# A two-layer expert kernel: the second layer of all three token blocks by seven half-width products

## The chip, the cores and the metric

The program runs on one core of a Trainium2 chip. The metric is device time in microseconds (us) from launch to end, the median of several executions; one more execution was recorded by the hardware profiler, and what is read below comes from that one. The engines are called TensorE (PE in the profile; its weight loads PEld), VectorE (DVE), ScalarE (ACT), GpSimd (POOL) and SyncE (SP, which issues the transfers).

## The reference

Gated linear attention over 4 x 8 heads gives 3072 tokens of width 384; a softmax gate, balanced by eight Sinkhorn rounds, weights eight two-layer experts for every token.

```python
logits = x @ w_gate;  P = np.exp(logits - logits.max())
...                                   # 8 rounds of row and column scaling
for e in range(8):
    h = np.maximum(x @ w1[e], 0.0)    # 384 -> 1024
    out += P[:, e:e + 1] * (h @ w2[e])  # 1024 -> 384
```

All products are made of float16 matmuls: each factor is split into a high and a low part, and a product is three matmuls (high x high, low x high, high x low).

## The kernel before, in words

The first third of the program (to about 490 us) computes the attention, the gate, and experts 0 and 1 in the plain way. The change lies in the rest: experts 2 to 7, in 48 periods. A period (`ORDER`) is one expert, one half of the inner width (512 of 1024) and one of four groups of 768 tokens.

*First layer.* A fast matrix-product scheme forms the period's 3 x 3 by 3 x 2 block product from 15 products (`SLOTS`), six matmuls of 256 columns each, in six PSUM banks kb_A to kb_F. Between products ScalarE copies banks out (`copy`, tiles cp), VectorE adds them into others (`add`, `init`, `sum`), and in the end the banks hold the hidden values, which ScalarE rectifies into float16 high parts (kh, kah, kgh) and VectorE or GpSimd turn into low parts (kl, kal, kgl). `EVENTS` tells after which product each of these stands; numbers of 15 and over belong to the next period. Two 256-token pairs are also summed into kr and kf, the left factors (kg) of the fast scheme of the second layer.

*Second layer.* Of three token blocks, 0 and 1 are `paired`: two 128-token halves at once by seven half-width (192-column) products from sums of the left factors (ka, kg, kh) and of the weights (k2, k2s), 42 matmuls. Block 2 is `plain`: 24 matmuls of 384 columns. Results lie in kxps and kyps; VectorE combines them (both, acc), or ScalarE scales them (yt) and GpSimd adds them into acc. These matmuls are dealt out between the first-layer products of a later period by a budget (`drain`), `LAG` products behind.

*Weights.* While one half's four token groups run, the next half's weights are loaded and prepared: `prepare_w1` (sums k1s on GpSimd, high parts k1h on ScalarE, low parts k1l on VectorE, a maximum wmx on VectorE) and `prepare_w2` (k2s, k2h, k2l, k2sl likewise), each step tied to a product by a list of numbers. The period in which k1l and k2l are formed is called heavy below, the other light; they alternate.

Every engine's order is fixed by the order in which the code records its instructions (`pin` and `mm`), so an instruction that waits holds up all behind it on its engine.

Of the kernel before, what the change touches and what calls it, by code (L numbers as in the profile page):

```python
# [258 lines left out]
def fast(ctx, tc, qkf, vbd, wg, w1, w2, out, flag):  # L259
# [784 lines left out]
    def prepare_w2(e, j, plain_first=False):  # L1044
        raw = raw_weights(e, 2, j)
        yield

        def maxima_():
            pin(nc.vector.tensor_reduce(out=wmx[:, 1, 4 * e + j:4 * e + j + 1], in_=raw.rearrange("p a f -> p (a f)"), axis=AX.X, op=ALU.max, apply_absolute_value=True))

        def lows():
            for g in range(2):
                pin(nc.vector.scalar_tensor_tensor(out=wl[:, g], in0=raw[:, g], scalar=W2S, in1=wh[:, g], op0=ALU.mult, op1=ALU.subtract))
# [448 lines left out]
```

## Time and profile before

| | us |
|---|---|
| median of three runs | 1511.97 (1510.23 to 1512.18) |
| profiled execution | 1511.74, its span 1510.0 |
| TensorE busy | 1477.1 |
| VectorE busy | 1282.7 |
| ScalarE, GpSimd busy | 1002.8, 968.4 |

A span runs from the first to the last instruction. In a row of the order of time stand the start, the duration, engine and line, the operation, output and inputs by the program's names, and their shapes; neighbours on one engine may overlap by some tens of nanoseconds, so the distance of two starts is what one costs. "x2" merges two neighbours.

### The profile page before, as it was taken

How to read it: one execution, taken by the hardware profiler on the slowest of the kernel's cores; microseconds unless marked ns; L12 is line 12 of the kernel's file. 1: busy time of each engine (PE TensorE's matmuls, PEld its weight loads, DVE VectorE, ACT ScalarE, POOL GpSimd, SP SyncE). 2: the span in 40 equal slices, each digit the busy share in tenths (PEclk: the TensorE clock that was granted, in tenths of full speed). 3: DMA queues.
4: the chain of work that ended last, by engine and by line, in shares of the span. 5: the costliest groups of instructions: out<-in, count | busy, mean ns of one | idle time of the engine just before them, and what ended most of it. 6: DMA issues, size and time to landing. Idle time of an engine off the chain costs nothing.

```text
span 1510.0 us, 37891 instructions
## 1 busy us (share of the span) xinstructions
PE 1477.1 (98%) x15185; PEld 1213.1 (80%) x15185; DVE 1282.7 (85%) x2352; ACT 1002.8 (66%) x2103; POOL 968.4 (64%) x1154
## 2 busy tenths in 40 slices
PE   7999999999999999999999999999999999999997
PEld 5788877666665788888888888888888888888885
DVE  8878888986676888989999999889899989888765
ACT  6655555654344777777777777777777777777663
POOL 1254444446429456888888887888777777777543
PEclk9999999999999999999999999999999999999999
DMA  8455654541001101222112221111111011000011
GB/s 280 113 133 131 139 129 117 138 121 35 22 27 46 39 12 49 59 60 55 55 47 64 64 64 34 42 54 43 32 33 33 23 33 33 22 12 12 7 59 66
DMA packets 82794, 95.85 MB, mean 63 GB/s; under 512 B 49872, under 2 KB 66384, under 8 KB 82608
## 3 DMA queue, kind: packets, MB, share of 16 engines
q1 hardware_dynamic: 82608, 93.34, 22.2%
q8 instruction: 120, 1.97, 0.6%
q14 instruction: 66, 0.54, 0.1%
HBM read 69.53 MB, written 14.16 MB: 55 GB/s over the span
## 4 chain that ended last, share of the span: by engine, by line
PE 88%; DVE 7%; ACT 2%; issue 1%; POOL 1%; DMA 1%; DVEq 0%; POOLq 0%; ACTq 0%
PE kyps L287 21%; PE yps L287 13%; PE kxps L287 12%; PE hps L287 10%; PE kb_A L287 8%; PE kb_B L287 8%; PE kb_D L287 6%; PE kb_C L287 4%; PE kb_E L287 2%; PE kb_F L287 2%; PE kvps L287 1%; PE aps L287 1%; DMA w1r<-in_w_dram 1%; DVE kf L1375 1%; POOL k1s L1026 0%
## 5 line engine op out<-in xcount | busy, mean ns | idle before, releaser
L287 PEld LDWEIGHTS <-k1h 128*128 128x128 f16 x2880 | 282.1, 98 | 38.7 <-DVE kl L1392 0.5
L1220 POOL TENSOR_TENSOR acc<-acc,yt 128x384 f32<-128x384 f32 x175 | 203.2, 1168 | 105.7 <-ACT yt L1219 101.2
L1387 POOL TENSOR_TENSOR kgl<-kf,kgh 128x512 f16<-128x512 f32 x188 | 217.1, 1165 | 40.9 <-ACT kgh L1384 40.2
L1219 ACT ACTIVATE yt<-kyps,pes 128x384 f32<-128x384 f32 x175 | 103.7, 592 | 131.8 <-PE kyps L287 69.6
L287 PEld LDWEIGHTS <-kh 128*128 128x128 f16 x1536 | 147.3, 98 | 34.8 <-DVE acc L1212 1.5
L287 PEld LDWEIGHTS <-k1l 128*128 128x128 f16 x1440 | 141.1, 98 | 24.6 <-issue 3.6
L287 PEld LDWEIGHTS <-kgh 128*128 128x128 f16 x1536 | 144.3, 98 | 5.3 <-ACT kgh L1384 1.1
L287 PE MATMUL yps<-w2h,hl 128*128 128x384 f16 x384 | 125.5, 327 | 2.8 <-DVE hl L440 2.6
L287 PE MATMUL yps<-w2l,hh 128*128 128x384 f16 x384 | 125.4, 326 | 1.9 <-DVE w2l L359 1.9
L287 PE MATMUL kyps<-k2h,kh 128*128 128x384 f16 x384 | 125.2, 326 | 1.5 <-DVE acc L1212 1.2
L287 PE MATMUL yps<-w2h,hh 128*128 128x384 f16 x384 | 125.5, 327 | 0.2 <-ACT hh L437 0.2
L287 PE MATMUL kyps<-k2h,kl 128*128 128x384 f16 x384 | 125.2, 326 | 0.4 <-DVE kl L1392 0.4
L287 PE MATMUL kyps<-k2l,kh 128*128 128x384 f16 x384 | 125.2, 326 | 0.0
L287 PEld LDWEIGHTS <-w1h 128*128 128x128 f16 x1344 | 97.2, 98 | 34.0 <-issue 3.1
L1384 ACT ACTIVATE kgh<-kf 128x512 f16<-128x512 f32 x192 | 120.7, 629 | 3.6 <-DVE kf L1375 3.5
L1254 POOL TENSOR_TENSOR part<-part 128x192 f32<-128x192 f32 x96 | 57.3, 596 | 88.7 <-DVE kf L1375 61.1
L287 PEld LDWEIGHTS <-hh 128*128 128x128 f16 x768 | 74.6, 98 | 47.7 <-issue 2.5
L1353 ACT ACTIVATE cp<-kb_A 128x512 f32<-128x512 f32 x144 | 87.4, 607 | 21.9 <-PE kb_A L287 21.6
L287 PE MATMUL kyps<-k2sl,kgh 128*128 128x192 f16 x384 | 94.5, 246 | 0.0
L287 PE MATMUL kyps<-k2sh,kgl 128*128 128x192 f16 x384 | 94.5, 246 | 0.0
L287 PE MATMUL kyps<-k2sh,kgh 128*128 128x192 f16 x384 | 94.5, 246 | 0.0
L287 PEld LDWEIGHTS <-kl 128*128 128x128 f16 x768 | 75.1, 98 | 23.3 <-issue 5.3
(294 smaller groups left out, 5404.3 us busy)
## 6 DMA issues: line engine op xcount, KB each, us to landing
q<-in_qkf_dram SPq DMA_DIRECT2D x23, 672.0 KB, 5.1
vr<-in_vbd_dram SPq DMA_DIRECT2D x24, 384.0 KB, 3.6
k1r<-in_w_dram SPq DMA_DIRECT2D x24, 384.0 KB, 3.0
ys<-yr SPq DMA_DIRECT2D x48, 192.0 KB, 2.7
k2r<-in_w_dram SPq DMA_DIRECT2D x24, 384.0 KB, 3.1
yb<-ys SPq DMA_DIRECT2D x48, 192.0 KB, 2.6
out_dram<-acc SPq DMA_DIRECT2D x24, 192.0 KB, 1.9
w1r<-in_w_dram SPq DMA_DIRECT2D x8, 384.0 KB, 7.7
```

The lines of the kernel that those rows point to most:

```text
L287: ins = (nc.tensor.transpose if transpose else nc.tensor.matmul)(**kw)
L1219: pin(nc.scalar.activation(out=yt, in_=ps, func=AF.Copy, scale=p))
L1220: pin(nc.gpsimd.tensor_tensor(out=y, in0=y, in1=yt, op=ALU.add))
L1254: pin(nc.gpsimd.tensor_tensor(out=part[:, 1, :], in0=part[:, 1, :], in1=part[:, 2, :], op=ALU.add))
L1353: pin(nc.scalar.activation(out=fresh(ev[2]), in_=bk, func=AF.Copy))
L1375: pin(nc.vector.scalar_tensor_tensor(out=f[:, n], in0=bk[:, :, 128 * v:128 * v + 128], scalar=0.0, in1=other, op0=ALU.max, op1=op))
L1384: pin(nc.scalar.activation(out=hs['g', t][0][:, lo:hi], in_=hs['f', t][:, lo:hi], func=AF.Copy))
L1387: pin((nc.vector if tag == str(PERIODS - 1) else nc.gpsimd).tensor_tensor(out=hs['g', t][1][:, lo:hi], in0=hs['f', t][:, lo:hi], in1=hs['g ...
```

## The change

All three blocks of the second layer are `paired`; `plain` is gone. The seven products now stand in the schedule by number (five first-layer products to a block, `advance`), six products behind the first layer instead of two. The scheme inside a block is rewritten with two running sums instead of a GpSimd chain: three ScalarE copies into PSUM (kxps, kyps) or part, then four scaled adds of 192 columns into acc, or into yy and xx that GpSimd adds to acc; kxps takes a bank of its own. The first layer gets along with five banks, kb_A and kb_F of a period lying in one. The third block's left factors come from kb_D and kb_F (`hs`, `gs`, `gd`), and every kal is formed by VectorE from its bank (`gf`). The weights' tile k2 now holds seven half-width parts.

```diff
-PLAIN, PAIRED = (2,), (0, 1)
+PAIRED = (0, 1, 2)
+BY_POOL = (1,)
-LAG = 2
+LAG = 6
...
-    pk = ctx.enter_context(tc.tile_pool(name="pk", bufs=6, space=PSUM, reuse_waits="tile"))
+    pk = ctx.enter_context(tc.tile_pool(name="pk", bufs=1, space=PSUM, reuse_waits="tile"))
...
+        product(y0, None, (0, 0), start=True)
+        product(x1, (None, 0), (None, 0))
+        yield
+        move(x0, y0)
+        move(p2, x1, scale=scale(1))
+        yield
+        product(y0, (None, 2), (None, 2))
+        yield
+        move(x1, y0)
+        yield
+        product(x0, (1, 0), (1, 0), stop=True)
+        yield
+        yield
+        product(x1, (None, 1), (None, 1))
+        yield
+        out_x(0, x0)
+        add(yy[:, 1, :], x1, scale(1), p2)
+        yield
+        product(y0, (1, 1), (None, 3), stop=True)
+        product(x1, (None, 3), (1, 1), stop=True)
+        yield
+        add(yy[:, 0, :], y0, scale(1), p2)
+        out_x(1, x1)
...
-            at_all(n, (10, 12, 18, 22, 23, 26, 26, 27, 38) if n != 3 else (0, 2, 8, 12, 13, 16, 16, 17, 20), prepare_w2(e2, 2 * m2 + part // 2))
-        if 3 <= n:
+            at_all(n, (10, 22, 25, 26, 27, 29, 35, 38) if n != 3 else (0, 2, 8, 12, 13, 16, 17, 20), prepare_w2(e2, 2 * m2 + part // 2))
+        if n >= FIRST_READD:
...
+    def kbank(n, bk):
+        k = "AFEC".find(bk)
+        tag = bk if k < 0 else f"k{(max(k - 1, 0) + int(n)) % 3}"
+        return pk.tile([128, 2, 256], F32, name=f"kb_{n}_{bk}", tag=tag)
...
+    def advance(n, s):
+        k, j = divmod(n * PRODUCTS + s - LAG, 5)
+        k -= TT
+        if k >= 0 and not j and k < PERIODS * TT:
+            going.append(paired(k // TT, helped[k // TT], PAIRED[k % TT]))
+        if not going or j == 1 and len(going) == 1 and k < PERIODS * TT:
+            return lambda: None
+        block = going[0 if j == 1 else -1]
+        next(block)
```

The first place that the prediction speaks of is VectorE's order in a heavy period (the 24th), from the add into kb_B to the making of kb_F. Before:

```order
L1355 TENSOR_TENSOR kb_B<-kb_B,cp_0_16334 128x512
L1039 SCALAR_TENSOR_TENSOR k1l_1_16087<-k1s_1_16001,k1h_1_16086 128x640 x2
L1039 SCALAR_TENSOR_TENSOR k1l_1_16087<-k1r_1_15843,k1h_1_16086 128x256
L1039 SCALAR_TENSOR_TENSOR k1l_1_16087<-k1r_1_15843,k1h_1_16086 128x384
L1375 SCALAR_TENSOR_TENSOR kf_0_16370<-kb_A,kr_0_16373 128x256
L1381 SCALAR_TENSOR_TENSOR kal_0_16390<-kb_A,kah_0_16389 128x256
L1355 TENSOR_TENSOR kb_D<-kb_D,cp_7_16414 128x512
L1053 SCALAR_TENSOR_TENSOR k2l_1_16265<-k2r_1_16072,k2h_1_16264 128x384
L1358 TENSOR_TENSOR kb_F<-kb_D,cp_1_16288 128x512
```

And now, from behind the add into kb_B on:

```order
L1182 SCALAR_TENSOR_TENSOR yy_2_16895<-kyps_2_16892,pes,part_2_16894 128x192
L1182 SCALAR_TENSOR_TENSOR acc_8993<-kyps_2_16892,pes,acc_8993 128x192
L1039 SCALAR_TENSOR_TENSOR k1l_1_16728<-k1s_1_16583,k1h_1_16727 128x640
L1047 TENSOR_REDUCE wmx<-k2r_1_16754 128x1
L1039 SCALAR_TENSOR_TENSOR k1l_1_16728<-k1s_1_16583,k1h_1_16727 128x640
L1039 SCALAR_TENSOR_TENSOR k1l_1_16728<-k1r_1_16496,k1h_1_16727 128x256
L1039 SCALAR_TENSOR_TENSOR k1l_1_16728<-k1r_1_16496,k1h_1_16727 128x384
L1332 SCALAR_TENSOR_TENSOR kal_0_17090<-kb_A,kah_0_17089 128x256
L1182 SCALAR_TENSOR_TENSOR acc_9363<-kxps_0_17016,pes,acc_9363 128x192
L1182 SCALAR_TENSOR_TENSOR yy_0_17018<-kyps_0_17015,pes,part_0_17017 128x192
L1302 TENSOR_TENSOR kb_D<-kb_D,cp_7_17112 128x512
L1305 TENSOR_TENSOR kb_F<-kb_D,cp_1_16975 128x512
```

Two scaled adds of the third block stand ahead of the k1l, the second layer's maximum stands between them, two more adds stand ahead of kb_D, and k2l has gone further down.

The second place is VectorE right behind kb_F in the same period, up to the low part of kb_D. Before:

```order
L1375 SCALAR_TENSOR_TENSOR kf_0_16370<-kb_B,kr_0_16373 128x256
L1375 SCALAR_TENSOR_TENSOR kf_0_16370<-kb_B,kf_0_16370 128x256 x2
L1364 TENSOR_TENSOR cp_3_16501<-kb_D,cp_4_16212 128x512
L1392 SCALAR_TENSOR_TENSOR kl_1_0_16179<-kb_B,kh_1_0_16178 128x512
L1257 TENSOR_TENSOR both_1_16444<-kyps_1_16442,part_1_16443 128x192
L1355 TENSOR_TENSOR kb_C<-kb_C,cp_3_16501 128x512
L1392 SCALAR_TENSOR_TENSOR kl_1_2_16183<-kb_D,kh_1_2_16182 128x512
```

And now, from k2l on:

```order
L1064 SCALAR_TENSOR_TENSOR k2l_1_17124<-k2r_1_16754,k2h_1_17123 128x192
L1064 SCALAR_TENSOR_TENSOR k2l_1_17124<-k2r_1_16754,k2h_1_17123 128x384
L1302 TENSOR_TENSOR kb_C<-kb_C,cp_3_17223 128x512
L1182 SCALAR_TENSOR_TENSOR yy_1_17139<-kyps_1_17136,pes,part_1_17138 128x192
L1351 SCALAR_TENSOR_TENSOR kl_2_16863<-kb_D,kh_2_16862 128x512
L1326 TENSOR_TENSOR kr_2_17286<-kr_2_17286 128x256
L1323 SCALAR_TENSOR_TENSOR kr_2_17286<-kb_D,kr_2_17286 128x256
L1323 SCALAR_TENSOR_TENSOR kf_2_17318<-kb_D,kr_2_17286 128x256
L1323 SCALAR_TENSOR_TENSOR kf_2_17318<-kb_D,kf_2_17318 128x256
```

k2l stands here now, and four instructions on the third block's left factors (kr, kf) follow the low part of kb_D, three of them reading that bank.

The third place is GpSimd's order beside it. Before:

```order
L1387 TENSOR_TENSOR kgl_1_16233<-kf_1_16231,kgh_1_16232 128x512 x2
L1220 TENSOR_TENSOR acc_9256<-acc_9256,yt_0_1_16349 128x384
L1071 TENSOR_TENSOR k2s_1_16353<-k2r_1_16072 128x192 x2
L1074 TENSOR_TENSOR k2s_1_16353<-k2r_1_16072,k2s_1_16353 128x192 x2
L1291 TENSOR_TENSOR acc_9594<-acc_9594,yz_6_1_16394 128x384
```

And now:

```order
L1346 TENSOR_TENSOR kgl_22_2_17054<-kr_2_16908,kgh_22_2_17052 128x512
L1218 TENSOR_TENSOR acc_8993<-acc_8993,yy_2_16895 128x384
L1346 TENSOR_TENSOR kgl_22_2_17055<-kf_2_16938,kgh_22_2_17053 128x512
L1326 TENSOR_TENSOR kr_0_17071<-kr_0_17071 128x256
L1239 TENSOR_TENSOR acc_8993<-acc_8993,yz_2_2_17101 128x384
L1057 TENSOR_TENSOR k2s_1_17155<-k2r_1_16754 128x192 x2
```

The two kgl of the third block and a kr are new there, and the weights' sums k2s come later.

More of the change, by code (lines that the diff above doesn't have):

```diff
@@ L1223, in product @@
-        def product(out, t, left, right, start=False, stop=False):
+        p = psm.tile([128, DM], F32, name=f"kyps_{n}_{t}", tag="m")
+        q = pk.tile([128, DM], F32, name=f"kxps_{n}_{t}", tag="x")
+        x0, y0, x1 = q[:, 0:DH], p[:, 0:DH], p[:, DH:DM]
+        p2 = lp.tile([128, DH], F32, name=f"part_{n}_{t}", tag="part", bufs=2)
+        by_pool = t in BY_POOL and n < len(ORDER) - 1 and not new
+        xx, yy = (acc[b][:, v, t, :].rearrange("p (s d) -> p s d", s=2) for v in range(2))
@@ L1224, in product, with scale @@
+        if not new:
+            yy = rp.tile([128, 2, DH], F32, name=f"yy_{n}_{t}", tag="yraw", bufs=3)
+        if by_pool:
+            xx = rp.tile([128, 2, DH], F32, name=f"xx_{n}_{t}", tag="yraw", bufs=3)
+        def scale(v):
+            return pes[:, (2 * b + v) * TT + t, e:e + 1]
+        def product(out, left, right, start=False, stop=False):
             for c in range(2):
@@ L1441, in fast @@
         period(n)
[L1442 to L1453 removed]
+    for s in range(LAG + PRODUCTS + 2):
+        for ev in pending.pop(0) if pending else []:
+            event(*ev)
+        advance(PERIODS, s)()
+        if s > 7:
+            next(judged, None)
+    if going:
+        raise RuntimeError("a block was left")
     for _ in again:
```

307 lines of the change are left out of this document (108 added, 199 removed), and 12 rows, old and new, of the table EVENTS.

## The prediction

> **What bounds the kernel now.** I read the page's totals first, then busy time by stretch, then TensorE's waits, then VectorE's and TensorE's order of time through one period.
>
> ```profile
> span 1510.0 us, 37891 instructions
> PE 1477.1 (98%) x15185; PEld 1213.1 (80%) x15185; DVE 1282.7 (85%) x2352; ACT 1002.8 (66%) x2103; POOL 968.4 (64%) x1154
> ```
>
> ```profile
> core 0: us, PE busy (x) PEld busy (x) DVE busy (x) ACT busy (x) POOL busy (x), PEclk, DMA share, GB/s
> 485.00:600.00 115.00, 107.38 (x960) 88.80 (x959) 91.38 (x169) 80.59 (x167) 62.80 (x87) 0.99 0.13 39
> 841.45:862.53 21.08, 21.08 (x206) 18.51 (x204) 20.20 (x37) 17.26 (x38) 18.19 (x21) 1.00 0.14 39
> 862.53:882.76 20.23, 20.23 (x196) 17.66 (x194) 17.40 (x34) 14.65 (x31) 16.39 (x24) 1.00 0.25 79
> 700.00:1100.00 400.00, 399.23 (x3831) 349.40 (x3829) 360.29 (x676) 307.88 (x657) 327.68 (x402) 1.00 0.17 49
> 1485.00:1510.00 25.00, 14.09 (x136) 11.27 (x133) 15.49 (x37) 7.98 (x19) 7.98 (x10) 0.94 0.19 69
> ```
>
> From 700 to 1100 TensorE lacks 0.8 us in 400, so matmul pitch sets the time there. VectorE is at 90% on average, but unevenly: in the period 841.45 to 862.53, where low parts of new weights are formed (a heavy period), it is busy 20.20 us; in the next, a light one, 17.40. The two together last 41.3 us, 20.65 each. The reserve in a heavy period is what this forecast turns on.
>
> ```profile
> 852.43 0.27 PE L287 MATMUL kb_A<-xbh,k1h 128*128 128x256 f16 x1
> 853.09 0.33 PE L287 MATMUL kyps<-k2h,kh 128*128 128x384 f16 x1
> 853.90 0.27 PE L287 MATMUL kb_E<-xah,k1h 128*128 128x256 f16 x1
> 847.91 0.25 PE L287 MATMUL kxps<-k2sl,kgh 128*128 128x192 f16 x1
> 848.73 0.27 PE L287 MATMUL kb_D<-xah,k1h 128*128 128x256 f16 x1
> 861.25 0.27 PE L287 MATMUL kb_D<-xah,k1h 128*128 128x256 f16 x1
> ```
>
> Pitches by starts: six 256-column matmuls stand between the first two rows (0.66/6 = 0.109 us), five of 384 between the next (0.81/5 = 0.162), ten of 192 from 847.91 to 848.73 (0.082).
>
> ```profile
> 850.20 0.36 DVE L1257 TENSOR_TENSOR both<-kyps,part 128x192 f32<-128x192 f32 x1
> 850.47 0.69 DVE L1358 TENSOR_TENSOR kb_E<-kb_D,cp 128x512 f32<-128x512 f32 x1
> 851.07 0.68 DVE L1392 SCALAR_TENSOR_TENSOR kl<-kb_C,kh 128x512 f16<-128x512 f32 x1
> 851.67 0.36 DVE L1260 TENSOR_TENSOR kxps<-kxps,both 128x192 f32<-128x192 f32 x1
> 852.06 0.62 DVE L1216 SCALAR_TENSOR_TENSOR acc<-kxps,pes,acc 128x384 f32<-128x384 f32 x1
> 852.70 0.57 DVE L1263 TENSOR_TENSOR kyps<-kyps,both 128x384 f32<-128x384 f32 x1
> 853.18 0.69 DVE L1355 TENSOR_TENSOR kb_B<-kb_B,cp 128x512 f32<-128x512 f32 x1
> 853.77 2.35 DVE L1039 SCALAR_TENSOR_TENSOR k1l<-k1s,k1h 128x640 f16<-128x640 f32 x2
> 854.51 1.62 DVE L1039 SCALAR_TENSOR_TENSOR k1l<-k1s,k1h 128x640 f16<-128x640 f32 x1
> 856.05 1.67 DVE L1039 SCALAR_TENSOR_TENSOR k1l<-k1r,k1h 128x256 f16<-128x256 f32 x2
> 857.65 0.41 DVE L1375 SCALAR_TENSOR_TENSOR kf<-kb_A,kr 128x256 f32<-128x256 f32 x1
> 857.98 0.41 DVE L1381 SCALAR_TENSOR_TENSOR kal<-kb_A,kah 128x256 f16<-128x256 f32 x1
> 858.31 0.68 DVE L1355 TENSOR_TENSOR kb_D<-kb_D,cp 128x512 f32<-128x512 f32 x1
> 858.91 1.30 DVE L1053 SCALAR_TENSOR_TENSOR k2l<-k2r,k2h 128x384 f16<-128x384 f32 x1
> 860.14 0.69 DVE L1358 TENSOR_TENSOR kb_F<-kb_D,cp 128x512 f32<-128x512 f32 x1
> 860.74 0.75 DVE L1053 SCALAR_TENSOR_TENSOR k2l<-k2r,k2h 128x384 f16<-128x384 f32 x1
> 861.41 0.41 DVE L1375 SCALAR_TENSOR_TENSOR kf<-kb_B,kr 128x256 f32<-128x256 f32 x1
> 861.75 0.87 DVE L1375 SCALAR_TENSOR_TENSOR kf<-kb_B,kf 128x256 f32<-128x256 f32 x2
> 862.53 0.68 DVE L1364 TENSOR_TENSOR cp<-kb_D,cp 128x512 f32<-128x512 f32 x1
> ```
>
> VectorE overlaps neighbours, so I use starts here too: 0.60 for 512 columns, 0.33 for 256, 0.27 for 192. The deadline is kb_F: it is made from kb_D and ends at 860.83, and TensorE writes kb_D again at 861.25, 0.42 us later. In the whole run that wait came twice:
>
> ```profile
> PE kb_D L287 <- DVE kb_F L1358: 1.4, 2, 1.0
> ```
>
> The four k1l instructions from 853.77 don't cost what their size says. The groups by tile (minimum/median/maximum ns) and GpSimd's order of time show why:
>
> ```profile
> L1039 DVE SCALAR_TENSOR_TENSOR k1l<-k1s,k1h x48: 810/846/1624, 451.0 to 1392.8; 128x640 f16<-128x640 f32 x48
> L1220 POOL TENSOR_TENSOR acc<-acc,yt x175: 988/1002/1712, 606.1 to 1501.8; 128x384 f32<-128x384 f32 x175
> L1387 POOL TENSOR_TENSOR kgl<-kf,kgh x188: 1146/1158/1870, 503.8 to 1474.2; 128x512 f16<-128x512 f32 x188
> L1049 DVE TENSOR_REDUCE wmx<-k2r x24: 941/942/947, 496.8 to 1376.8; 128x1 f32<-128x768 f32 x24
> 853.96 1.48 POOL L1220 TENSOR_TENSOR acc<-acc,yt 128x384 f32<-128x384 f32 x1 [0.18 <-ACT yt L1219]
> ```
>
> The first k1l runs alone (0.74 to the next start, 0.81 long) and GpSimd's add beside it is stretched to 1.48; the second k1l stands 1.62, until that add is over. They take turns. So each such VectorE instruction waits out at most the one GpSimd instruction before it. Alone the four take 0.74 + 0.74 + 0.34 + 0.48 = 2.3 us by their columns; here 3.88, so 1.58 of waiting. The maxima (TENSOR_REDUCE) never stretch. The Trainium skill, GPSIMD Engine Reference, Key points, says that GpSimd shares its SBUF interfaces with VectorE instructions that have two SBUF inputs or a 2-port mode; the rows agree.
>
> **The change, part by part.** *TensorE.* Per period 24 matmuls of 384 columns give way to 42 of 192: 24 x 0.162 = 3.89 against 42 x 0.0825 = 3.46, a gain of 0.425 us, and 20.4 us over 48 periods. A period becomes 90 x 0.109 + 126 x 0.0825 = 20.2 us. (0.0825 is 0.66 for eight, between the row's 0.082 and the period's average.)
>
> *VectorE, per period.* Out: both, kxps, acc, kyps of two blocks, 2 x (0.27 + 0.39 + 0.53 + 0.48) = 3.3 (acc is 0.62 long, less the 0.09 by which a 512-wide one overlaps its successor); the low part of kb_F (0.60); kf and kal from kb_A and kb_E, 4 x 0.33 = 1.3. In: ten scaled adds of 192 columns, for which 0.27 (192, no scale) and 0.33 (256) are the bounds; I take 0.33, as the scaled 384-wide row is 0.05 longer than the plain one; so 3.3; three kr/kf steps on kb_D (1.1 by 861.41 to 862.53), three kal (1.0), one kr subtract (0.3). Net +0.5. Of the weights' work, the second layer's maxima (0.9) move from the light into the heavy period, and k2l goes from two of 384 (1.23 + 0.67) to one of 192 and one of 384 (0.8 alone, at most 1.9). So a heavy period asks 20.20 + 0.5 + 0.9 - 1.9 + 1.35 = 21.05 us of VectorE, and TensorE would be through in 20.2; a light one asks 17.4 + 0.5 - 0.9 = 17.0. The overload is 0.85 before any wait in order is counted; the next period absorbs it only if no bank is due.
>
> *The first deadline, kb_F.* Counted from the end of a period's eighth first-layer product plus the twelve 192-wide ones behind it, where the third block's last add can start: 0.2 (a product's row is 0.25 long, its pitch 0.08) + 0.33 for that add; then k1l, maxima, k1l, k1l, k1l: 2.3 + 0.9; kal 0.33; two scaled adds 0.66; kb_D 0.60; kb_F 0.69. Sum 6.0 us. TensorE has five first-layer products (30 x 0.109) and seven half-width ones (42 x 0.0825) until it writes kb_D: 6.74. Alone it fits by 0.7. With the old 1.58 of turn-taking it is 0.9 late; if GpSimd always has an instruction ready, the last three k1l wait out most of an acc add, a kgl of 1.16 and a kr of 128 x 256 (0.7 by its columns), about 2.0 in all, and it is 1.3 late. Behind kb_F wait TensorE's whole queue and all that reads it.
>
> *The second deadline, kb_D and kb_A.* kb_D now feeds three kr/kf steps, all before the next period's fifth product; from kb_F on VectorE needs 7.1 us (k2l alone) to 8.2, TensorE 7.9. Then kb_A's add and its copy on ScalarE: 8.7 to 9.9 us, due at 9.0. So 0 to 0.9 more. By the skill's rule the kr subtract on VectorE, with two SBUF inputs, would take turns as well: an estimate of up to 1.2 more, which I leave in the upper bound.
>
> I take 1.5 us lost per heavy period, between 0.9 and 2.2. There are 20 with both first- and second-layer weights in them (n from 5 to 43): 30 us.
>
> *GpSimd.* Out per period: part and both (four of 192 columns, 2 us by the 1.0 of 384); in: two more kgl (2.3) and two kr (1.3); adds into acc stay four. It is busy 82% now (16.9 per period) and nears 92% of 20.2: not the bound, but nearly always able to take a turn, which feeds the k1l waits. VectorE's kr/kf steps on kb_B now wait for GpSimd's kr, and its adds into yy for a buffer that GpSimd's acc add frees; both have several products of cover, so I cost them at nothing; without it the hl parts and TensorE's next kb_B would be late by one GpSimd instruction, 1.2. *SP*: the early outputs' 48 loads move two periods later with one buffer for two; each has three products (about 4 us) to land, hidden; else ScalarE's copies behind it wait. *ScalarE*: 77% busy; two more 512-wide, one more 256-wide and five more 192-wide copies, four of 384 fewer; its copies wait on the banks above and are hidden otherwise.
>
> *Start and end.* Layer 2 starts four products later. The stretch 485 to 600 already lacks 7.6 us of TensorE; one more is taken (bounds -2 and +4). At the end 10.9 us are lacking; the last period's three blocks run alone as two did, and I take zero (-3 to +3).
>
> *Sum.* The profiled execution's own time is 1511.74 us, at the runs' median of 1511.97. 1511.7 - 20.4 + 30 + 1 = 1522.
>
> **The rivals.** *Heavy periods fit (faster).* If GpSimd is idle, or its instructions fall elsewhere, so that the k1l wait less than 0.7 us, kb_F is in time and nothing is lost: 1511.7 - 20.4 + 1 = 1492, with 0.4 lost per heavy period 1500. For it: before, the same work ended 0.42 early with 1.58 of turns. Against: the maxima are added at just that place. It decides at 1.0 us lost per heavy period.
>
> *An even trade.* 0.9 to 1.1 lost: 1509 to 1515.
>
> *Both deadlines missed.* 1.3 + 0.9 per heavy period: 1492 + 44 = 1536; with the kr subtract also taking turns, 2.7, 1546.
>
> *Half-width matmuls held to their weight loads.* The load takes 98 ns by its row:
>
> ```profile
> L287 PEld LDWEIGHTS <-kgh 128*128 128x128 f16 x1536 | 144.3, 98 | 5.3 <-ACT kgh L1384 1.1
> ```
>
> Were each 192-wide matmul spaced by that, 42 x 0.098 = 4.1 against 3.89, and the change would cost 0.2 per period, 1522 without any VectorE wait. The 0.082 pitch in this very kernel speaks against it: loads overlap. The Trainium skill's TensorE: Matmul & The Clock Gate, Back-to-back issue gap, gives 81 ns at 128 columns and 131 at 512 for sustained streams; an estimate between them is 89 ns at 192 and 114 at 384, which would make the change 48 us slower, to 1560. The rows show 82 and 162, so that rule does not hold here.
>
> **How the numbers follow.** Forecast (1515 to 1531) 0.35; fits 0.35 (1492 to 1508); even trade 0.12; both deadlines 0.17; weight loads 0.01. Cases of both signs hold most of the chance; the forecast's own range is that in brackets. A measurement of this kernel tells about 0.2% from no change, 1509 to 1515. So faster 0.35, same 0.12, slower 0.53. The range 1494 to 1542 leaves out a little of the best and of the worst case.
>
> **What would show it.** Right: waits of TensorE's kb_D on VectorE's kb_F once per heavy period, a second, smaller group on kb_D's kf or kb_A's copy, light periods at 20.2 us, VectorE over 92% from 700 to 1100. Wrong: TensorE still without idle time in the middle (then 1492 to 1496); waits on GpSimd's kgl or kr instead; or a first 100 us of layer 2 that lacks far more than 9 us.

## The result and the profile after

The changed kernel takes 1562.8 us (1561.54 to 1563.76, four runs) against 1512.05 before: a ratio of 1.034, 95% interval 1.032 to 1.036. It is 51 us slower where 10 were forecast. In the profiled execution the granted clock is 0.995 of full speed and TensorE is busy 5 us longer, so the difference is waiting.

The page's totals:

```profile
span 1561.0 us, 40193 instructions
PE 1481.7 (95%) x16051; PEld 1263.9 (81%) x16051; DVE 1328.4 (85%) x2558; ACT 1037.1 (66%) x2310; POOL 1032.2 (66%) x1149
```

Busy time by stretch (length, then PE, PEld, DVE, ACT, POOL, clock, DMA). The first two run from one first matmul into kb_F to the next, the third is the middle, the fourth goes from the last kb_F to the end:

```profile
1034.92:1057.45 22.53, 21.01 (x219) 19.06 (x217) 20.54 (x40) 15.87 (x38) 18.58 (x19) 1.00 0.13 37
1057.45:1078.65 21.20, 20.71 (x219) 19.16 (x217) 18.54 (x37) 17.78 (x40) 18.57 (x26) 1.00 0.20 57
700.00:1100.00 400.00, 378.98 (x3921) 346.64 (x3919) 362.54 (x710) 302.91 (x699) 337.67 (x383) 1.00 0.18 51
1527.75:1561.04 33.29, 18.42 (x205) 16.86 (x203) 21.73 (x57) 9.77 (x25) 4.19 (x5) 0.91 0.21 75
```

From 700 to 1100 TensorE now lacks 21.0 us in 400, where it lacked 0.8. I call a stretch from one kb_F to the next *heavy* if a heavy period's kb_F ends it, so that the k1l lie in it, and *light* if a light period's does: 22.53 and 21.20 here, where both were 20.65 before. Of the 51 us, 41.5 lie in the 47 stretches (981.4 us before, 1022.9 after), 8.1 behind the last kb_F (25.2 and 33.3), 1.4 ahead of the first.

TensorE's waits in the whole run (total, times, longest):

```profile
PE kyps L287 <- DVE yy L1182: 21.0, 25, 2.0
PE kb_A L287 <- DVE kal L1332: 9.0, 20, 1.2
PE kb_A L287 <- ACT cp L1300: 8.2, 30, 1.1
PE kb_B L287 <- ACT cp L1300: 5.1, 21, 1.4
PE kb_D L287 <- DVE kb_F L1305: 4.6, 22, 0.7
```

The wait that I named, kb_D on kb_F, is there 22 times, but of these five it is the smallest. The largest stands ahead of it in the same queue. VectorE's order of time in a heavy period, with TensorE's two waiting matmuls behind it:

```profile
1048.84 0.41 DVE L1182 SCALAR_TENSOR_TENSOR acc<-kyps,pes,acc 128x192 f32<-128x192 f32 x1
1049.16 0.81 DVE L1039 SCALAR_TENSOR_TENSOR k1l<-k1s,k1h 128x640 f16<-128x640 f32 x1
1049.89 0.94 DVE L1047 TENSOR_REDUCE wmx<-k2r 128x1 f32<-128x768 f32 x1
1050.76 0.82 DVE L1039 SCALAR_TENSOR_TENSOR k1l<-k1s,k1h 128x640 f16<-128x640 f32 x1
1051.49 2.38 DVE L1039 SCALAR_TENSOR_TENSOR k1l<-k1r,k1h 128x256 f16<-128x256 f32 x2
1053.79 0.41 DVE L1332 SCALAR_TENSOR_TENSOR kal<-kb_A,kah 128x256 f16<-128x256 f32 x1
1054.13 0.40 DVE L1182 SCALAR_TENSOR_TENSOR acc<-kxps,pes,acc 128x192 f32<-128x192 f32 x1
1054.45 0.40 DVE L1182 SCALAR_TENSOR_TENSOR yy<-kyps,pes,part 128x192 f32<-128x192 f32 x1
...
1055.50 0.70 DVE L1305 TENSOR_TENSOR kb_F<-kb_D,cp 128x512 f32<-128x512 f32 x1
...
1054.91 0.24 PE L287 MATMUL kyps<-k2h,kh 128*128 128x192 f16 x1 [0.70 <-DVE yy L1182]
...
1056.25 0.27 PE L287 MATMUL kb_D<-xah,k1h 128*128 128x256 f16 x1 [0.19 <-DVE kb_F L1305]
```

The yy add reads one half of the bank kyps; TensorE's next product writes the other half and waits for it. The four k1l and the maximum hold that add up; the product comes two half-width products ahead of kb_D, so it is the earlier deadline.

More is lost behind kb_F. VectorE's order at the start of the same heavy stretch, with TensorE's next kb_A:

```profile
1034.97 0.42 DVE L1323 SCALAR_TENSOR_TENSOR kr<-kb_B,kr 128x256 f32<-128x256 f32 x1 [0.32 <-POOL kr L1326]
...
1036.10 0.41 DVE L1332 SCALAR_TENSOR_TENSOR kal<-kb_E,kah 128x256 f16<-128x256 f32 x1
...
1036.57 0.28 PE L287 MATMUL kb_A<-xbh,k1h 128*128 128x256 f16 x1 [0.41 <-DVE kal L1332]
...
1039.58 1.42 DVE L1326 TENSOR_TENSOR kr<-kr 128x256 f32<-128x256 f32 x1 [0.35 <-ACT kr L1315]
```

And in the light stretch behind it, with the two waits that TensorE's rows list there:

```profile
1059.40 1.59 DVE L1064 SCALAR_TENSOR_TENSOR k2l<-k2r,k2h 128x192 f16<-128x192 f32 x2
...
1062.44 0.97 DVE L1326 TENSOR_TENSOR kr<-kr 128x256 f32<-128x256 f32 x1
...
1063.32 0.27 PE L287 MATMUL kb_B<-xah,k1h 128*128 128x256 f16 x1 [0.17 <-ACT cp L1300]
1066.28 0.27 PE L287 MATMUL kb_A<-xbh,k1h 128*128 128x256 f16 x1 [0.23 <-ACT cp L1300]
```

With five banks, the next kb_A takes the bank of this period's kb_E, whose last reader is kal, and kal stands behind three kr/kf steps that wait for GpSimd. The 20 waits for kal in the list all lie in heavy stretches. The suspects in the light ones are k2l and the kr subtract: VectorE instructions with two SBUF inputs, longer than their columns. The kr subtract on VectorE is 0.97 us long in light and 1.42 in heavy stretches while the early outputs (those of experts 0 and 1, loaded again and added into acc) are being added, to about 1140 us, and 0.41 to 0.43 in every later period.

A matmul's row (0.27 us) is longer than its pitch, so the idle time in brackets is less than what is lost. The distances of TensorE's starts, less the pitches of 0.0825 and 0.109 us, show where a stretch loses against 20.2. A light one loses 0.40 us at kb_A (for its copy by ScalarE), 0.34 at kb_B (likewise) and 0.25 at kb_D (for kf) while early outputs are added: all of its 1.0. A heavy one loses 0.85 at yy, 0.57 at kal and 0.35 at kb_F, and while early outputs are added 0.40 at kb_A's copy too.

### The profile page after: what moved, and what is told of

Its sections match the earlier page's. It is cut to its first block, busy times and chain, and to the rows that moved or that the text cites. A ratio compares the mean times of both kernels' runs of the same rounds, so it can differ in the third digit from the quotient of the medians.

```text
span 1561.0 us, 40193 instructions
## 1 busy us (share of the span) xinstructions
PE 1481.7 (95%) x16051; PEld 1263.9 (81%) x16051; DVE 1328.4 (85%) x2558; ACT 1037.1 (66%) x2310; POOL 1032.2 (66%) x1149
## 4 chain that ended last, share of the span: by engine, by line
PE 46%; DVE 31%; POOL 12%; issue 5%; ACT 5%; DMA 0%; POOLq 0%; DVEq 0%; ACTq 0%
PE yps L287 12%; PE hps L287 10%; PE kyps L287 9%; POOL kgl L1346 5%; POOL k1s L1026 5%; PE kb_A L287 4%; DVE k1l L1039 4%; PE kb_B L287 4%; DVE kf L1323 4%; DVE yy L1182 2%; DVE kr L1323 2%; DVE kr L1326 2%; DVE k2l L1064 2%; DVE kl L1351 2%; DVE acc L1182 2%
## 5 line engine op out<-in xcount | busy, mean ns | idle before, releaser
L287 PEld LDWEIGHTS <-k1h 128*128 128x128 f16 x2880 | 281.3, 98 | 51.7 <-DVE kal L1332 14.9
L287 PE MATMUL kyps<-k2h,kgh 128*128 128x192 f16 x1152 | 283.6, 246 | 1.0 <-ACT kyps L1179 1.0
L287 PE MATMUL kyps<-k2h,kgl 128*128 128x192 f16 x1152 | 283.6, 246 | 0.0
L287 PE MATMUL kyps<-k2l,kgh 128*128 128x192 f16 x1152 | 283.5, 246 | 0.0
L287 PEld LDWEIGHTS <-kgh 128*128 128x128 f16 x2304 | 216.8, 98 | 3.2
L1346 POOL TENSOR_TENSOR kgl<-kr,kgh 128x512 f16<-128x512 f32 x141 | 168.8, 1197 | 58.6 <-ACT kgh L1343 58.6
L1182 DVE SCALAR_TENSOR_TENSOR yy<-kyps,pes,part 128x192 f32<-128x192 f32 x264 | 108.3, 410 | 85.8 <-PE kyps L287 83.3
L1218 POOL TENSOR_TENSOR acc<-acc,yy 128x384 f32<-128x384 f32 x129 | 141.3, 1096 | 42.1 <-DVE yy L1182 42.1
L287 PEld LDWEIGHTS <-kgl 128*128 128x128 f16 x1152 | 112.8, 98 | 4.6 <-issue 1.2
L287 PE MATMUL kb_A<-xbh,k1h 128*128 128x256 f16 x288 | 78.6, 273 | 17.1 <-DVE kal L1332 9.0
L287 PE MATMUL kyps<-k2h,kh 128*128 128x192 f16 x288 | 70.7, 245 | 22.5 <-DVE yy L1182 21.0
L1343 ACT ACTIVATE kgh<-kr 128x512 f16<-128x512 f32 x144 | 90.7, 630 | 1.9 <-DVE kr L1323 1.8
```

The source lines that it names most:

```text
L287: ins = (nc.tensor.transpose if transpose else nc.tensor.matmul)(**kw)
L1182: pin(nc.vector.scalar_tensor_tensor(out=y, in0=ps, scalar=p, in1=z, op0=ALU.mult, op1=ALU.add))
L1218: pin((nc.vector if n == len(ORDER) - 1 else nc.gpsimd).tensor_tensor(out=y, in0=y, in1=z.rearrange("p s d -> p (s d)"), op=ALU.add))
L1343: pin(nc.scalar.activation(out=hs['g', t][0][i], in_=hs['f' if i else 'r', t], func=AF.Copy))
L1346: pin((nc.vector if tag == str(PERIODS - 1) else nc.gpsimd).tensor_tensor(out=hs['g', t][1][i], in0=hs['f' if i else 'r', t], in1=hs['g', ...
```

## The experiments

All are edits of the changed kernel. The table gives each time, its ratio to the kernel before, and from its trace the median light and heavy stretch, while early outputs are added (n from 5 to 28) and after (29 to 42), and the time behind the last kb_F. Here n is the period whose kb_F begins the stretch. A step is the work that is recorded behind the first-layer product of that number. From both_moves on, all but no_k1_lows contain the edit of kal_first.

| run | us | ratio (95%) | light, heavy to n = 28 | light, heavy after | end |
|---|---|---|---|---|---|
| before | 1511.9 | | 20.65, 20.65 | 20.65, 20.65 | 25.2 |
| after | 1562.8 | 1.034 (1.032 to 1.036) | 21.20, 22.56 | 20.84, 22.10 | 33.3 |
| kal_first | 1553.0 | 1.027 (1.026 to 1.029) | 21.19, 22.17 | 20.83, 21.76 | 33.3 |
| max_ahead | 1562.6 | 1.034 (1.032 to 1.036) | 21.20, 22.53 | 20.83, 22.07 | 33.4 |
| both_moves | 1552.1 | 1.027 (1.025 to 1.029) | 21.19, 21.74 | 20.83, 21.74 | 33.1 |
| no_k1_lows | 1539.4 | 1.018 (1.017 to 1.020) | 21.55, 21.35 | 21.18, 20.90 | 32.2 |
| k1l_ahead | 1541.7 | 1.020 (1.018 to 1.021) | 21.19, 21.61 | 20.83, 21.10 | 33.4 |
| kr_gpsimd | 1568.5 | 1.038 (1.036 to 1.040) | 21.60, 22.97 | 20.75, 21.72 | 32.9 |
| k1l_kr2 | 1576.0 | 1.043 (1.041 to 1.044) | 21.48, 22.21 | 21.64, 22.21 | 33.7 |
| no_kgl | 1534.3 | 1.015 (1.014 to 1.017) | 20.64, 22.32 | 20.22, 21.52 | 29.4 |
| kr_bank | 1593.6 | 1.055 (1.053 to 1.056) | 21.66, 22.90 | 21.86, 22.88 | 33.7 |
| kr_bank_k1l28 | 1602.0 | 1.060 (1.058 to 1.062) | 23.70, 21.71 | 22.90, 21.70 | 33.9 |
| kr_banks_k1l | 1586.7 | 1.050 (1.048 to 1.051) | 21.67, 22.89 | 21.87, 22.32 | 32.3 |
| kr_first | 1541.3 | 1.020 (1.018 to 1.021) | 20.55, 21.76 | 20.75, 21.75 | 33.7 |
| kr_first_k1l | 1526.3 | 1.010 (1.008 to 1.012) | 20.55, 21.06 | 20.75, 21.05 | 33.3 |
| krs_first_k1l | 1532.7 | 1.014 (1.013 to 1.016) | 21.05, 21.12 | 20.75, 21.16 | 31.0 |
| kr_first_k1l28 | 1548.6 | 1.025 (1.023 to 1.026) | 22.59, 20.55 | 21.78, 20.54 | 33.1 |
| k1l_spread | 1522.0 | 1.007 (1.005 to 1.009) | 20.55, 21.05 | 21.00, 20.64 | 31.5 |
| k1l_k2l_spread | 1522.2 | 1.007 (1.005 to 1.009) | 21.07, 20.73 | 21.17, 20.32 | 30.6 |
| all_spread | 1518.8 | 1.005 (1.004 to 1.006) | 20.22, 21.38 | 20.38, 20.91 | 30.9 |

**kal_first.** The low part from kb_E ahead of the kr/kf steps.

```diff
-13: (('gs', 'B', 0, 1), ('gs', 'B', 0, 2), ('gs', 'B', 0, 3), ('gf', 'E', 1), ('gd', 1, 'P')),
+13: (('gf', 'E', 1), ('gs', 'B', 0, 1), ('gs', 'B', 0, 2), ('gs', 'B', 0, 3), ('gd', 1, 'P')),
```

> Only the order of VectorE's work in step 13 is changed: the low part formed from kb_E (kal) runs ahead of the three kr/kf steps on kb_B. Theory 1, a bank in order: TensorE's next kb_A takes the bank of this period's kb_E, and waits every period for this kal, 0.39 us in heavy and 0.57 in light periods (21.7 us over 45 places). Moved ahead it ends some 1.1 us (heavy) to 1.4 us (light) earlier, these waits go, and the time is near 1562.8 - 21 = 1542. Theory 2, VectorE's load: where VectorE is short of time an earlier kal only makes other steps later; light periods gain 0.57 x 24 = 13 us, heavy ones nothing, 1550. Theory 3, the prediction's (only kb_F in heavy periods counts): no change, 1561 to 1565.

9.8 us less. TensorE's waits for kal are gone. They had not lain in every period, as the expectation says, but in heavy stretches alone, and light ones keep their 21.19, with the same waits at kb_B, kb_D and kb_A. Heavy ones fall to 21.77 in two of three; up to n = 28 the others stay at 22.5 to 22.8 (but for one of 24.2), and the 22.17 of the table is only the middle between the two levels. In the high ones the kr subtract takes 1.75 to 1.78 us, in the low ones 0.64 or 0.65. Theory 2 had the sum about right and the places the wrong way round: the gain is in the heavy stretches. What holds the light ones stands elsewhere in the queue.

**max_ahead.** The maximum of heavy periods ahead of the block's last adds, in VectorE's idle time.

```diff
+            next(ahead.pop((n, s), iter(())), None)   # ahead[n + 1, 7]: the step of prepare_w2 that forms wmx
             rest()
```

> In heavy periods the second-layer maximum (0.87 us from start to start) runs ahead of the last adds of the block in step 7, into a stretch in which VectorE stands idle about 1.2 to 1.4 us for TensorE; the four k1l stay behind those adds. Theory 1, the deadline at step 12: TensorE's product into kyps waits 0.9 us per heavy period for VectorE's add into yy, which stands behind k1l and this maximum; 0.87 x 20 = 17 us go, and with part of the 0.35 x 20 waits of kb_D on kb_F up to 23: 1540 to 1546. Theory 2, the prediction's kb_F deadline alone: 7 us, 1556. Theory 3, VectorE's or GpSimd's load over the whole period: under 4 us, 1559 to 1563, since no work is taken away.

No change. VectorE's order of time shows why:

```profile
1047.03 0.94 DVE L1047 TENSOR_REDUCE wmx<-k2r 128x1 f32<-128x768 f32 x1
...
1049.21 2.36 DVE L1039 SCALAR_TENSOR_TENSOR k1l<-k1s,k1h 128x640 f16<-128x640 f32 x2
1051.49 2.37 DVE L1039 SCALAR_TENSOR_TENSOR k1l<-k1r,k1h 128x256 f16<-128x256 f32 x2
1053.79 0.41 DVE L1338 SCALAR_TENSOR_TENSOR kal<-kb_A,kah 128x256 f16<-128x256 f32 x1
```

The maximum ran ahead of the block's last adds, and from the first k1l to kal it is 4.58 us, where it was 4.63: the four k1l now fill that time without it. In the changed kernel the maximum (1049.89 to 1050.83) ran while GpSimd had its turn:

```profile
1049.20 1.63 POOL L1218 TENSOR_TENSOR acc<-acc,yy 128x384 f32<-128x384 f32 x1
1050.80 1.79 POOL L1346 TENSOR_TENSOR kgl<-kf,kgh 128x512 f16<-128x512 f32 x1
```

The next k1l had to sit that turn out anyway, so the maximum had cost nothing. My sum charged it 0.9.

**both_moves.** Both edits.

> Both reorderings together. If the two waits are separate places in the queue (theory 1 twice), the gains add up: 1562.8 - 21 - 17 = 1525, between 1518 and 1530. If a load stands behind them (VectorE's in heavy periods, or GpSimd's, whose kr VectorE's kr/kf steps wait for), the second adds less than half of its own gain: 1533 to 1542.

The second adds 0.9 us; alone it had brought 0.2. That is under half of the 17 expected of it alone, and neither forecast holds: 1552.1 lies above both.

**no_k1_lows.** No k1l; TensorE reads the high parts twice.

```diff
-                pin(nc.vector.scalar_tensor_tensor(out=wl[:, at_, :], ...))
+                pass
```

> Leaves out the k1l instructions (the first-layer weights' low parts; TensorE reads the high parts in their place, as many matmuls as before). This prices those four instructions, 2.3 us by columns and 3 to 4 us with the turns that they take with GpSimd. Theory 1 (the heavy periods lose by what stands ahead of the yy and kb_F adds): heavy periods become as long as light ones, 22.55 to 21.2 us, 20 x 1.35 = 27 us less, 1536; the waits at kb_A stay. Theory 2 (GpSimd's load sets the heavy period, its kgl and kr come late): less than half of that, above 1548.

23 us less. Heavy stretches fall by 1.2 us to the level of the light ones, as theory 1 has it (the light ones rise by 0.35), and both still lose 0.7 to 1.35 us against 20.2: that half of the loss doesn't hang on k1l.

**k1l_ahead.** kal_first, and the first k1l (not the maximum) in the idle time of step 7.

```diff
-            at_all(n, (0, 3, 4, 5, 6, 8, 9, 10, 11, 22, 23, 24) ..., gen)
+            at_all(n, (0, 3, 4, 5, 6, 8, 9, 10, 11), gen)
+            ahead[n + 1, 7] = gen
+            at_all(n, (23, 24), gen)
```

> As kal_first (1553.0 us), and the first k1l of heavy periods runs ahead of the last adds of the block in step 7, where VectorE stands idle 1.4 us; the maximum and three k1l stay behind. Theory 1 (turns): what the maximum could not bring (it ran beside a GpSimd instruction for which the next k1l had to wait anyway), a k1l does, since each k1l ahead is one turn less behind: the yy add that TensorE's step 12 waits for comes 0.7 to 1.6 us earlier, the 0.8 us wait goes and part of the 0.35 at kb_F: 20 x 0.8 to 1.1 = 16 to 22, 1531 to 1537. Theory 2 (VectorE's load over the whole period, whatever the order): below 4 us, 1549 to 1553.

11.3 us less than kal_first, short of theory 1's 16 to 22, but nearly three times what theory 2 allows; most heavy stretches fall to 21.1, and the yy wait from 20.7 us to

```profile
PE kyps L287 <- DVE yy L1182: 8.6, 12, 2.0
```

So the same idle time that was worth nothing to a maximum is worth 0.65 us to a k1l: what counts is the number of turns behind.

**no_kgl.** kal_first without GpSimd's six kgl; TensorE reads kgh in their place.

```diff
-            pin((... nc.gpsimd).tensor_tensor(out=hs['g', t][1][i], in0=..., in1=hs['g', t][0][i], op=ALU.subtract))
+            hs['g', t][1][i] = hs['g', t][0][i]
```

> As kal_first (1553.0 us), but leaves out GpSimd's six kgl per period (TensorE reads kgh in their place, as many matmuls as before); VectorE's instructions and their order stay as they are. Theory 1 (turns): the four k1l wait mostly for kgl; without them they and the maximum need 3.2 to 3.8 us where they need 4.6, the yy add comes some 1 us earlier, and heavy periods fall from 21.77 to 20.6 to 20.9; light ones lose the turns of kr<-kr too. 1553 - 20 x 1.0 - 24 x 0.4 = 1523, between 1515 and 1530. Theory 2 (VectorE's own work is too long for the period): the same instructions remain, under 8 us, 1545 to 1553.

The time is between the two forecasts, and the split is the opposite of theory 1's: heavy stretches don't fall up to n = 28 (22.32 for a median of 22.17) and hardly after (21.52 for 21.76); light ones do, to 20.64, and to 20.22 once the early outputs are through. The kr subtract takes 0.41 to 0.43 us throughout. The k1l simply take turns with what comes next on GpSimd (VectorE above, GpSimd below):

```profile
992.07 1.51 DVE L1039 SCALAR_TENSOR_TENSOR k1l<-k1s,k1h 128x640 f16<-128x640 f32 x1
993.51 0.94 DVE L1047 TENSOR_REDUCE wmx<-k2r 128x1 f32<-128x768 f32 x1
994.37 1.45 DVE L1039 SCALAR_TENSOR_TENSOR k1l<-k1s,k1h 128x640 f16<-128x640 f32 x1
995.75 1.68 DVE L1039 SCALAR_TENSOR_TENSOR k1l<-k1r,k1h 128x256 f16<-128x256 f32 x2
...
991.91 1.00 POOL L1218 TENSOR_TENSOR acc<-acc,yy 128x384 f32<-128x384 f32 x1 [4.40 <-DVE yy L1182]
992.86 1.31 POOL L1326 TENSOR_TENSOR kr<-kr 128x256 f32<-128x256 f32 x1
994.13 1.01 POOL L1239 TENSOR_TENSOR acc<-acc,yz 128x384 f32<-128x384 f32 x1
995.09 1.91 POOL L1057 TENSOR_TENSOR k2s<-k2r 128x192 f32<-128x192 f32 x2
```

Here the first two k1l last 1.51 and 1.45 us, where they had 0.81 and 0.82, because GpSimd starts an add or subtract just ahead of each; what VectorE does is the same, and it needs 5.3 us for it in place of 4.6. After n = 28, without the early outputs' adds, it needs 4.5. The light stretches of 20.22 show that TensorE's floor of 20.2 us is real.

**kr_gpsimd and k1l_kr2.** The VectorE kr subtract on GpSimd; then with k1l_ahead too, and the steps on kb_D behind the add into kb_A.

```diff
-('gd', 2, 'V')
+('gd', 2, 'P')
```

> As kal_first (1553.0 us), and the kr subtract of the third block (kr<-kr 128x256), which VectorE does in 1.0 to 1.4 us while it takes turns with GpSimd, goes to GpSimd, which stands idle for 2.4 us at that time. After it TensorE waits three times in each light period (kb_B 0.33, kb_D 0.24, kb_A 0.4). If these come from this subtract ahead of the kr/kf steps on kb_D, yy and the add into kb_A, VectorE gains up to 1.0 us per period, but kr/kf must now wait for GpSimd, some 0.35 us later than VectorE ended: 0.3 to 0.7 us per light period, 1535 to 1546. If GpSimd's queue is the limit (its two kgl stand ahead), kr comes later than before and the time rises, 1555 to 1565.

> Both of the other two reorderings, and the kr/kf steps on kb_D stand behind the next period's add into kb_A, so that this add no longer waits for GpSimd's kr. If the waits are separate places in the queues: heavy and light periods near 20.5 us, 1562.8 - 47 x 1.35 - 2 = 1500 at best, 1505 to 1525 if the ends of the period keep 0.3 us each. If VectorE's load stands behind it: 1530 or more.

Both are slower (by 15 and 34 us than kal_first and k1l_ahead): GpSimd does it behind its two kgl, and TensorE waits for kb_D instead, whose reader comes late. That is the second forecast's cause for kr_gpsimd, at more than its price (1555 to 1565). In k1l_kr2:

```profile
PE kb_D L287 <- DVE kf L1328: 45.1, 47, 2.2
```

My second edit had put those readers even further back; the bank has a deadline of its own, which that edit left out of account.

**kr_bank, kr_first.** The subtract stays on VectorE but reads one operand from the bank kb_F. In kr_bank it stands behind ScalarE's kah<-kb_F, in kr_first ahead of it.

```diff
-            pin((...).tensor_tensor(out=r[:, 0], in0=r[:, 1], in1=r[:, 0], op=ALU.subtract))
+            pin(nc.vector.scalar_tensor_tensor(out=r[:, 0], in0=banks_["AEF"[ev[1]]][:, :, 128:256], scalar=0.0, in1=r[:, 0], op0=ALU.max, op1=ALU.subtract))
...
-17: (('ga', 'F', 2), ('gd', 2, 'V'), ...
+17: (('gd', 2, 'V'), ('ga', 'F', 2), ...   # kr_first
```

> As kal_first (1553.0 us), and VectorE's kr subtract of the third block reads one operand from the bank kb_F instead of from SBUF (relu of the bank minus the other half, the same value, 256 columns). Theory 1 (turns): with two SBUF inputs it takes 0.97 to 1.42 us because it waits for GpSimd's kgl; from the bank it should take the 0.33 pitch of the kr/kf steps beside it, so the kr/kf steps on kb_D, the yy add and the add into kb_A come 0.6 to 1.0 us earlier, and the waits of 0.33 + 0.24 + 0.4 us after them shrink by at least half in every period: 47 x 0.5 to 0.8, 1515 to 1530. Theory 2 (GpSimd's own lateness: its kr for the first block, its kgl for TensorE): the subtract isn't what is waited for, under 6 us, 1547 to 1553.

> As kr_bank, but the subtract that reads the bank kb_F stands ahead of ScalarE's kah<-kb_F in the program: in kr_bank VectorE stood idle 2.15 us until that ScalarE instruction was over, so that run tested a new wait and not the turns. Against kal_first (1553.0 us): theory 1 (the 0.97 to 1.42 us of kr<-kr, its turns with GpSimd, make the kr/kf steps on kb_D, the yy add and the add into kb_A late): light periods fall from 21.19 and 20.83 to 20.4 to 20.7, heavy by as much; 47 x 0.4 to 0.7, 1520 to 1535. Theory 2 (ScalarE's kr<-kb_F and kah set these steps, or GpSimd's kgl set TensorE's start): under 6 us, 1547 to 1553.

kr_bank is 40.6 us slower than kal_first. VectorE's own waits name the new one:

```profile
DVE kr L1329 <- ACT kah L1332: 71.3, 48, 2.1
```

ScalarE and VectorE both only read kb_F, and still VectorE waits for ScalarE, once per period. The Trainium skill, PSUM — Partial Sum Buffer, PSUM bank collisions raise a hardware error, says that two engines must be kept out of one bank, on the same partitions, at the same time, reads included. The program's waits here do that. Two more runs carry this wait (71.7 and 77.7 us) and price little else. kr_bank_k1l28 has k1l_ahead too, and the last two k1l at step 13: 1508 to 1525 or 1528 to 1545 us were expected, and it took 1602.0. kr_banks_k1l has k1l_ahead and the first block's subtract on VectorE from kb_A: 1503 to 1518 or at least 1525 were expected, and it took 1586.7. Both come again below without the wait.

With the order turned, kr_first is 11.7 us faster than kal_first, short of theory 1's range (1520 to 1535) and well over theory 2's 6. The subtract by groups (minimum/median/maximum ns), in the changed kernel and in kr_first:

```profile
L1326 DVE TENSOR_TENSOR kr<-kr x48: 407/746/1432, 510.9 to 1532.9; 128x256 f32<-128x256 f32 x48
```

```profile
L1329 DVE SCALAR_TENSOR_TENSOR kr<-kb_F,kr x48: 404/414/425, 511.2 to 1511.2; 128x256 f32<-128x256 f32 x48
```

It is never longer than 425 ns now, and light stretches fall from 21.19 to 20.55: two thirds of their loss. The waits at kb_A and kb_D are gone there, and 0.33 at kb_B is left. Where it was 0.42 already (n from 29) they gain 0.08.

**kr_first_k1l, kr_first_k1l28, krs_first_k1l.** kr_first with k1l_ahead; then the last two k1l at step 13; or the first block's subtract on VectorE from kb_A, with GpSimd forming kgl of two blocks in the last period.

```diff
-                at_all(n, (23, 24), gen)
+                at_all(n, (23, 28), gen)          # kr_first_k1l28
...
-9: (('ga', 'A', 0), ('gd', 0, 'P')),
+9: (('gd', 0, 'V'), ('ga', 'A', 0)),              # krs_first_k1l
```

> kr_first and k1l_ahead together (k1l_ahead: 1541.7 us, heavy periods 21.1). If the two losses are separate (one behind the k1l, one behind the kr subtract), their gains add up: 1541.7 - 47 x 0.4 to 0.7, 1509 to 1523. If one covers the other: 1530 or more.

> As kr_first_k1l, and the last two k1l move from step 9 to step 13 of heavy periods, behind kb_F. Theory 1: kb_D's wait on kb_F (0.35 us, 20 times) goes, and what kr_first gained pays for them behind: 3 to 8 us less than kr_first_k1l. Theory 2: behind kb_F they make the kr/kf steps on kb_D and the add into kb_A late: 10 to 25 us more than kr_first_k1l.

> As kr_first_k1l, with the first block's kr subtract on VectorE too, from kb_A, ahead of kah (0.33 us of VectorE in place of 0.7 of GpSimd), and with GpSimd forming kgl of two blocks in the last period. If GpSimd's load is what light periods still lose by (20.83 against 20.22 when its kgl were left out), another 0.1 to 0.3 us per period goes, 5 to 14 us, and the tail behind the last kb_F is 2 to 4 us shorter. If VectorE's columns count, periods become 0.1 to 0.3 us longer, and only the tail gains.

The two gains add up and a little more: 1526.3 is 26.7 less than kal_first, where they are 11.7 and 11.3 alone. It lies between the two forecasts, as the subtract's gain is smaller than expected. Two k1l behind kb_F bring the heavy stretch to 20.55 and the light one to 22.59: there they hold up kl, for which TensorE's kb_B waits 30.6 us in all. The subtract on VectorE costs more than it relieves GpSimd (6.3 us more), through the same wait for kl; only the end is 2.3 us shorter.

**k1l_spread, k1l_k2l_spread, all_spread.** From kr_first_k1l and the shorter end: the last two k1l at step 10, behind kal, acc and yy; then the two k2l of step 14 in the idle time of the next step 7; then the maximum over k1rm from step 9 to step 12.

```diff
-                at_all(n, (23, 24), gen)
+                at_all(n, (23, 25), gen)
...
-            at_all(n, (10, 22, 25, 26, 27, 29, 35, 38) ..., gen)
+            at_all(n, (10, 22, 25, 26, 27), gen)
+            ahead[n + 2, 7] = gen
+            at_all(n, (38, 40), gen)
...
-            at_slots(n, (1, 9), maxima)
+            at_slots(n, (1,), maxima)
+            ahead[n, 12] = maxima
```

> As kr_first_k1l (1526.3 us), with the last two k1l behind kal, acc and yy of step 10 and ahead of the add into kb_D, so that these three (bank operands) run while GpSimd has its turn; and in the last period GpSimd forms kgl of two blocks again (in krs_first_k1l the stretch behind the last kb_F was 31.0 in place of 33.3 us). Theory 1 (turns can be covered by instructions that read banks): the rest of the yy wait (0.2 us) goes and kb_F comes up to 1 us earlier, heavy periods from 21.05 to 20.5 to 20.8; 20 x 0.4 + 2.3: 1513 to 1520. Theory 2 (the turns only move): 21.05 stays, 1523 to 1526 by the tail alone.

> As k1l_spread, and the two k2l of step 14 in heavy periods (1.58 us with their turns, ahead of the add into kb_C) run ahead of the last adds of step 7 of the next light period, where VectorE stands idle 1.2 us; ScalarE's and VectorE's work on the sums follows two to three steps later. Theory 1: TensorE's waits for kb_B (0.35 us behind ScalarE's copies, once per pair of periods) go, heavy or light periods lose 0.3 us less, 7 us: 1507 to 1515. Theory 2 (light periods have no room either): the k2l of the sums, now ahead of kb_D and kb_F, makes light periods 0.3 to 1 us longer, 1525 to 1545.

> As k1l_k2l_spread (1522.2 us), and in light periods the maximum over the first experts' weights (k1rm, 0.86 us, for which VectorE stands idle 1.03 us in step 9 until its load lands) runs in step 12 instead, behind kb_F and ahead of the block's last adds. Theory 1 (place in the queue): TensorE's wait of kb_D for kb_F in light periods, 0.85 us, goes, since kb_F comes up to 1.9 us earlier: 21.07 to about 20.4 us in some 16 light periods, 10 us less: 1509 to 1514, level with the kernel before (1511.9) or just under it. Theory 2 (VectorE's load): the maximum makes the steps behind kb_F late by as much: 1518 to 1524.

k1l_spread gains 4.3, of which 1.7 at the end (33.3 to 31.5). Up to n = 28 the heavy stretch keeps its 21.05, so there the turns only moved, as theory 2 has it; after, it falls by 0.41, and the light one rises by 0.25. k1l_k2l_spread gains nothing more and lies between its two forecasts. Heavy stretches lose 0.3 less, and light ones wait 0.85 for kb_F, behind a maximum whose load is late:

```profile
1050.46 0.95 DVE L1080 TENSOR_REDUCE wmx<-k1rm 128x1 f32<-128x768 f32 x1 [1.03 <-DMA k1rm<-in_w_dram]
```

The light stretches' 0.33 at kb_B is gone in this run: TensorE's wait there for ScalarE's copy is listed 21 times in k1l_spread and once here. all_spread takes the wait for kb_F away, light stretches reach TensorE's floor of 20.22, and heavy ones rise by 0.65, from a new wait of kb_B on kl, as theory 2 has it, whose range the time falls into:

```profile
PE kb_B L287 <- DVE kl L1366: 10.8, 18, 2.6
```

Its 47 stretches take 981.1 us, as long as before (981.4), though TensorE could be through in 950 at 20.22 each. The whole is still 0.5% slower than the kernel before, since the start (2.5 us longer) and the end (30.9 us against 25.2) are not made up. No version beat it.

## Why the prediction was wrong

The time came 41 us above the forecast. Against 20.22 us each, the 20 heavy stretches lose 45, where 30 were forecast; the 20 light ones from n = 5 on lose 17, where at most the second deadline's part of those 30 belongs; and the end takes 8 more. About 1 is left to the first four stretches and the start.

*TensorE's gain: right.* 20.2 us per period were worked out from pitches; 20.22 is the light stretch of no_kgl and of all_spread. The weight loads don't hold the matmuls.

*Heavy periods, 1.5 us each: the mechanism right, the place and the size wrong.* Against 20.2 they lose 2.35 us (1.9 after n = 28). The step that failed here is the choice of kb_F as the first deadline. By the numbers that stood there, the yy add needs kb_F's 6.0 less the 0.60 and 0.69 of kb_D and kb_F, 4.7 us, and is due two half-width products (0.99) ahead of kb_D, at 5.75: with 1.6 to 2.0 of turns, 0.55 to 0.95 late. By the starts of its matmuls TensorE is 0.85 late there, and 0.35 more at kb_F. I had counted that add in the sum and not asked who waits for it. The 0.9 for the maximum was wrong as well (max_ahead); the turns made up for it.

*Light periods at 20.2 us: wrong, and so in every rival.* They lose 1.0 us (0.64 after n = 28). Shown: up to n = 28 about two thirds are the kr subtract that takes turns (kr_first). For this I had named "an estimate of up to 1.2 more" and left it out of the sum for all 48 periods, at 0.3 us in place of 0.97 and 1.42; the upper bound of 2.2 (1.3 + 0.9) doesn't hold it either, and the rival's 2.7 holds 0.5 of it. The other 0.33, at kb_B, goes when the two k2l are moved (k1l_k2l_spread), an edit that leaves the maximum over k1rm where it was.

*The second deadline, kb_D and kb_A: the place right, its cause and its periods wrong.* Behind a heavy period's kb_F, which is the light stretch, TensorE waits 0.25 us at kb_D and 0.40 at kb_A's copy, within the 0 to 0.9 forecast. But kr_first, which leaves k2l where it is, ends both, so the kr subtract makes them late; and the 0.40 comes behind light periods' kb_F as well. The group on kb_A's copy is larger than that on kb_F (8.2 and 4.6 us in all), not smaller.

*The bank of kb_E: missed.* The prediction followed what feeds each bank, not which bank the next period's kb_A inherits. Its wait is 0.57 us by TensorE's starts. Taking it away (kal_first, 9.8 us in all) shortens a heavy stretch by 0.34 us after n = 28, as 0.28 comes back at kb_B; up to n = 28 by 0.75 to 0.97 in half of them and by nothing in the others.

*GpSimd's waits, costed at nothing: wrong in part.* The wait of kr/kf on kb_B for GpSimd's kr (0.32) had the cover I named for TensorE's kb_B, but stood ahead of kal in VectorE's queue.

*Start and end, +1: too small.* The start has +1.4; the end was taken as zero within 3 and has +8.1. TensorE is busy 18.4 us behind the last kb_F, where the 25 us before had 14.1, I take it because the second layer now follows six products behind, which no run tests; and it idles 14.9 in place of 10.9.

*The rivals.* Both deadlines missed (1536, or 1546 with the subtract taking turns) was nearest, and still in heavy periods alone. That the wider pitches set aside with the weight-load rival would have given 1560 is chance: light stretches of 20.22 leave no room for them. Of what would show it, TensorE's idle time and kb_D's wait came; VectorE's 92% did not (362.54 of 400, 91%): VectorE held TensorE up in its order while it still had idle time.

*Where the middle's 41.5 us went* is shown: they come back by order and by one operand's place, with no instruction taken away. In all_spread about 31 us above TensorE's 20.22 each are still lost, 20 of them in the heavy stretches: up to n = 28, by TensorE's starts, 0.59 us each at kb_B for kl and 0.50 at kb_D for kb_F. Each run moved such a loss from one bank to another; whether an order without any exists stays open.

## What to carry to other kernels

For each bank of accumulators, list who reads it last and which matmul writes it next, also when the reader uses another half of the bank, and check every one of these against the queue of the reading engine; every bank's deadline counts, and the earliest in program order is worked out first. An instruction of VectorE with two SBUF inputs is priced with the GpSimd instruction that may stand ahead of it, in every period; one that reads a bank, or a maximum, is not. A maximum in the place where a turn is waited out cost nothing here; for steps on banks (k1l_spread) that showed only in part.
